# Splitting the rows of maxima with VectorE's tensor_reduce, and sending them in one transfer from ScalarE's queue

## The chip, the cores and the metric

The kernel runs on one core of a Trainium2 chip. A core has five engines with an instruction stream each, in order: TensorE (PE in the profile; its weight loads, PEld, overlap its matmuls), VectorE (DVE), ScalarE (ACT), GpSimd (POOL) and SyncE (SP), which here only issues DMA transfers. ScalarE can issue transfers too; such an issue then stands in ScalarE's stream, between its arithmetic instructions. The metric is the device time of one execution in microseconds; lower is better. Times come from several runs; one execution is also profiled.

## The reference

A transformer block with modulated layer norms: an attention with 16 heads of width 28 over 2048 tokens, and then a gated MLP whose gate is mixed over the tokens by a 2048 x 2048 matrix. Everything is float32.

```python
def _A_ref(x, wqkv, wo):
    B, S, D = x.shape            # 1, 2048, 448
    H = 16
    Dh = D // H                  # 28
    qkv = (x @ wqkv).reshape(B, S, 3, H, Dh).transpose(2, 0, 3, 1, 4)
    q, k, v = qkv[0], qkv[1], qkv[2]
    scores = jnp.einsum("bhqd,bhkd->bhqk", q, k) * (Dh ** -0.5)
    p = _softmax(scores, axis=-1)
    o = jnp.einsum("bhqk,bhkd->bhqd", p, v)
    return o.transpose(0, 2, 1, 3).reshape(B, S, D) @ wo

mod = (_silu(c) @ w_mod).reshape(c.shape[0], 6, 1, -1)
sa, ca, ga, sb, cb, gb = (mod[:, i] for i in range(6))
h = _layernorm(x, axis=-1) * (1 + ca) + sa
x = x + ga * _A_ref(h, A_wqkv, A_wo)
h = _layernorm(x, axis=-1) * (1 + cb) + sb
x = x + gb * _B_ref(h, B_w_in, B_w_sp, B_b_sp, B_w_out)
```

The change concerns the softmax alone: the maximum of each query's scores, which is subtracted before the exponential.

## The kernel before, in words

**Precision.** Operands of the big products are split into a high part in fp32r (a rounded float32 that TensorE multiplies in one pass) and a low part that holds the rest. For q and k of a head the parts are stacked over the partitions, so that one matmul of 128 rows gives the sum of the products.

**The attention.** The stack of a head h lies in `qst[h % 3]` and `kst[h % 3]`, 2048 columns each. Rows 0 to 83 hold the parts of q and k. Rows 84 and 85 of `qst` hold the negated maximum of each query, as a high and a low part, and the matching rows of `kst` hold ones: a score matmul that reads these rows has the maximum already subtracted, and ScalarE only applies exp. `load_head` (L669) loads a head's stack and first writes zeros to rows 84 and 85, because the maxima themselves are taken from the same stack without them.

The steps per head, by their names:

- `m_mm` (L747) computes 128 queries x 512 keys into PSUM (tile mt), and VectorE reduces this to one maximum per query (tile pm, L756). There are 64 of these for a head, or 48 where 4 of 16 blocks are covered by the next step.
- For the heads in `RAW`, 1 to 13, queries 0 to 511 are handled otherwise: `r_mm` (L789) computes their scores (tile rt) with keys on the partitions, ScalarE copies them to SBUF (rawA, rawB, rawC), VectorE keeps a running maximum (rmax, L802), and `r_turn` (L804) transposes rmax on TensorE and reduces it to columns 0 to 3 of tile mxv (L810).
- `m_max` (L760) reduces pm to the rest of mxv, negated, copies it to the high part of tile mxp (rounded to fp32r, L769) and subtracts that for the low part (L770, by the helper `sub` at L143). All three are VectorE instructions on 16 columns.
- `m_fin` (L772) transposes mxp on TensorE (tile mtp, L775), copies the result to SBUF (tile nt, 32 x 128, VectorE, L778) and issues two transfers on the sync queue, of 16 rows of 128 each, into rows 84 and 85 of the head's stack (L780).
- For the heads in `RAW`, `r_neg` (L812) reads those rows: a matmul spreads the negated maxima over all partitions (L814), ScalarE copies this to tile rneg (L818), and GpSimd adds it to each raw tile (`r_sub`, L821), after which ScalarE applies exp (`x_exp`).
- `s_mm` (L833) computes the other scores (st_ps, L786) and their exp (tile P, L831). `pv_mm` (L845) multiplies P with V (o_ps, L850).

**The order.** It is written out by hand. `pair(u)` (L1118) issues two key blocks at a time by a string such as `rrpm|smsmssmsmsm`: r is an `r_mm`, p is `pv_mm` of the pair before and then the steps listed as `late`, | runs the second block's events, s is an `s_mm` and m an `m_mm`. Eight such pairs make a head. `n_o` counts the r and s issued so far in the pair. `m_max` of head h stands among the events at the start of pair 16h - 4, `m_fin` among the late steps in that pair's p, and `r_neg` at the | of the next pair. TensorE, in order, reaches `m_fin`'s transposition right behind the `pv_mm`s of that p.

GpSimd adds, beside the attention, sums of blocks of the mixing matrix (`ws_op`, L946 to L960), whose loads and stores share the sync queue with everything else.

A planner, `Clock` (L1020), chooses which of seven PSUM banks each tile takes: it adds up estimated times of TensorE, ScalarE and VectorE (`clock.read`, `clock.spend`) and picks the bank that comes free first. It changes no order.

Of the kernel before, what the change touches and what calls it, by code (L numbers as in the profile page):

```python
# [8 lines left out]
F32 = mybir.dt.float32  # L9
F32R = mybir.dt.float32r  # L10
AF = mybir.ActivationFunctionType
ALU = mybir.AluOpType
AX = mybir.AxisListType
# [6 lines left out]
NT = S // 128  # L20
# [69 lines left out]
def tile_adaln_mha_gmlp(ctx, tc, x, wqkv, wo, w_in, w_spT, b_sp, w_out, cT, w_mod, out):  # L90
    nc = tc.nc
    ctx.enter_context(tc.manual_schedule())
    pe, dve, act, pool, sp = nc.tensor, nc.vector, nc.scalar, nc.gpsimd, nc.sync
# [48 lines left out]
    def sub(eng, dst, a, hi):  # L142
        eng.tensor_tensor(out=dst, in0=a, in1=hi.bitcast(F32), op=ALU.subtract)  # L143
# [101 lines left out]
    def bank(name):  # L245
        k = mode[0](name) if mode[0] else banks[0]
        banks.remove(k)
        banks.append(k)
        return ring.tile([128, 512], F32, name=name, tag=f"b{k}")
# [6 lines left out]
    def load_mod(pair, eng):  # L256
        for k in range(4):
            n = 2 * D if k < 3 else 512
            wms[pair, k] = wm = e1.tile([128, 2 * D], F32, name="wm", tag=("wm", "wm", "raw")[pair], bufs=4)[:, :n]
            eng.dma_start(wm, w_mod[:, pair, 2 * D * k : 2 * D * k + n])  # L260
            if k < 3:
                wms[pair, k] = wm.rearrange("p (a b) -> p a b", b=D)
# [43 lines left out]
    for r0, r1, a, o in ((0, 128, 0, 3), (0, 64, 3, 1), (64, 128, 3, 1)):  # L306
        b = a + r0 // 64
# [343 lines left out]
    for g in range(1, NG):  # L651
        if g == 3:
# [3 lines left out]
            kst, qst = [a[0] for a in kq], [a[1] for a in kq]  # L656
            npool = att.enter_context(tc.tile_pool(name="npool", bufs=2))
# [73 lines left out]
    RAW = range(1, 14)  # L731
# [13 lines left out]
    pms = {}  # L745

    def m_mm(j, kb):  # L747
        h, t = divmod(j, NT)
        mt = bank("mt")
        pe.matmul(  # L750
            mt, qst[h % 3][:, t * 128 : (t + 1) * 128], kst[h % 3][:, kb * 512 : (kb + 1) * 512], start=True, stop=True
        )
        if h not in pms:
            pms[h] = npool.tile([128, NT, 4], F32, name="pm")
        clock.read("dve", 0.598)
        dve.tensor_reduce(out=pms[h][:, t, kb : kb + 1], in_=mt, axis=AX.X, op=ALU.max)  # L756

    mxs = {}

    def m_max(h):  # L760

        r = 4 if h in RAW else 0
        if h not in mxv:
            mxv[h] = npool.tile([128, NT], F32, name="mxv")
        mx = mxv.pop(h)
        clock.spend("dve", 0.4)
        dve.tensor_reduce(out=mx[:, r:], in_=pms.pop(h)[:, r:, :], axis=AX.X, op=ALU.max, negate=True)
        mxs[h] = npool.tile([128, 2, NT], F32R, name="mxp")
        dve.tensor_copy(mxs[h][:, 0, :], mx)  # L769
        sub(dve, mxs[h][:, 1, :], mx, mxs[h][:, 0, :])  # L770

    def m_fin(h):  # L772
        mx = mxs.pop(h)
        tp = bank("mtp")
        pe.transpose(tp[0 : 2 * NT, 0:128], mx.bitcast(F32).rearrange("p a b -> p (a b)"), ident)  # L775
        nt = npool.tile([2 * NT, 128], F32, name="nt", bufs=1)
        clock.read("dve", 0.3)
        dve.tensor_copy(nt, tp[0 : 2 * NT, 0:128])  # L778
        for i in range(2):
            sp.dma_start(qst[h % 3][84 + i : 85 + i, :].bitcast(F32), nt[NT * i : NT * (i + 1)])  # L780

    mxv, seen, rmax, rneg = {}, [], [], []

# [5 lines left out]
    def r_mm(u):  # L789
        st = score("rt", *divmod(u, NT), 0)  # L790
        b = clock.read("act", 0.477, hold=u % NT > 0)
        act.activation(raw_tile(u), st, AF.Copy)  # L792
        if u % NT:
            seen.append((u, st, b))

    def r_max():
        while seen:
            u, st, b = seen.pop(0)
            if not rmax:
                rmax.append(stage2.tile([128, 512], F32, name="rmax", tag="ql"))  # L800
            clock.read("dve", 0.6, *b)
            dve.tensor_tensor(out=rmax[0], in0=st, in1=raw_tile(u - 1) if u % NT == 1 else rmax[0], op=ALU.max)  # L802

    def r_turn(h):  # L804
        tp = bank("rtp")
        for t in range(4):
            pe.transpose(tp[:, t * 128 : (t + 1) * 128], rmax[0][:, t * 128 : (t + 1) * 128], ident)
        mxv[h] = npool.tile([128, NT], F32, name="mxv")
        clock.read("dve", 0.62)
        dve.tensor_reduce(out=mxv[h][:, 0:4], in_=tp.rearrange("p (a b) -> p a b", b=128), axis=AX.X, op=ALU.max, negate=True)  # L810

    def r_neg(h):  # L812
        st = bank("st_ps")
# [19 lines left out]
    def s_mm(u, qb):  # L833
        st = score("st_ps", *divmod(u, NT), qb)
        clock.ready[u] = clock.read("act", 0.477)[1]
        s_exp(u, qb, st)

    def x_exp(u):
        clock.ready[u] = clock.spend("act", 0.477)
        s_exp(u, 0, raw_tile(u))  # L840
# [4 lines left out]
    def pv_mm(u):  # L845
        h, kt = divmod(u, NT)
        if kt == 0:
            otile[h] = ps_o.tile([128, 512], F32, name="o_ps", tag="o")
        for qb in range(4):
            pe.matmul(  # L850
                otile[h][32 * qb : 32 * qb + 32, :], V[:, kt, h, :], ptiles.pop((u, qb)), start=kt == 0, stop=kt == NT - 1
            )
# [128 lines left out]
    for h in range(H):  # L981
        if h >= 2:
            at(h * NT - LEAD - 10, load_head, h)
        e0 = (h + 1) * NT
        at(e0 + 1, n_copy, h)
        at(e0 + 2, n_sum, h)
        at(e0 + 4, n_recip, h)
        at(e0 + 6, n_bcast, h)
        at(e0 + 8, n_mul, h)
        at(e0 + 9, n_scatter, h)  # L990
        at(h * NT + NT - LEAD, m_max, h)
        at(max(h * NT + NT - LEAD, -2), m_fin, h, when=late)
    for h in RAW:
        at(h * NT - 6, r_turn, h, when=late)
        at(h * NT - 1, r_neg, h)
        for k in range(NT):
            at(h * NT + (k // 2 - 1 if k < 4 else k - 3), r_sub, h * NT + k)
# [114 lines left out]
    def run(when, u):  # L1112
        for fn, a in when.pop(u, []):
            fn(*a)
# [3 lines left out]
    def pair(u):  # L1118
        ss = [[(v, qb) for qb in range(1 if v // NT in RAW else 0, 4)] if v < NU else [] for v in (u, u + 1)]
        S_, M_, R_ = ss[0] + ss[1], m_work[u] + m_work[u + 1], r_work[u] + r_work[u + 1]  # L1120
        X_ = [v for v in (u, u + 1) if v < NU and v // NT in RAW]
        xat = [len(R_) + 4, len(R_) + 6] if u % NT == 0 else [len(R_)] * 2
        if X_:
            order = ORDERS[8 if len(M_) > 6 else 6]
        else:
            lead = 1 if M_ else 4
            order = "r" * len(R_) + "s" * lead + "p" + "ms" * (4 - lead) + "|" + "ms" * 4 + "m" * len(M_)
        n_o = 0

        def exps():  # L1130
            while X_ and n_o >= xat[-len(X_)]:
                x_exp(X_.pop(0))

        run(events, u)
        exps()
        for c in order + "s" * len(S_) + "r" * len(R_) + "m" * len(M_):
            if c == "p":
                if u > 0:
                    pv_mm(u - 2)
                    pv_mm(u - 1)  # L1140
                    clock.pause((u - 2, u - 1))
                run(late, u)
            elif c == "|":
                run(events, u + 1)
            elif c == "s" and S_:
                s_mm(*S_.pop(0))
                n_o += 1
                exps()
            elif c == "r" and R_:
                r_mm(R_.pop(0))  # L1150
                n_o += 1
                exps()
                if not R_:
                    r_max()
            elif c == "m" and M_:
                m_mm(*M_.pop(0))
        assert not X_ and not seen
        run(late, u + 1)
# [102 lines left out]
    h = H - 1  # L1261
# [568 lines left out]
```

## Time and profile before

| What | Value |
|---|---|
| Median of 3 runs | 1381.62 us (1377.2 to 1386.27) |
| Profiled execution, device time | 1383.93 us |
| Its span | 1382.1 us |
| Granted TensorE clock, mean | 0.996 of full |
| TensorE busy | 1353.5 us, 98% |
| VectorE busy | 1099.5 us, 80% |
| ScalarE busy | 907.8 us, 66% |
| GpSimd busy | 603.8 us, 44% |
| 16 instances of the copy at L769 | 0.174 us least, 5.910 us most |
| TensorE's wait at `m_fin`'s transposition (L775) | 15.1 us in 9 heads |
| TensorE's wait for the rows at `r_neg` (L814) | 2.77 us in 1 head |

The shares are of the whole span; the stretch of the change is the attention, from about 130 to 870 us. A row of a timeline gives start, duration, engine, line, operation, output <- input, and in brackets the idle time of the engine just before it with what ended that. Merged rows ("x6") give the time from the first start to the last end. SPq and ACTq are the queues' issues of transfers. The device time of the profiled execution is 1.8 us above its span.

### The profile page before, as it was taken

How to read it: one execution, taken by the hardware profiler on the slowest of the kernel's cores; microseconds unless marked ns; L12 is line 12 of the kernel's file. 1: busy time of each engine (PE TensorE's matmuls, PEld its weight loads, DVE VectorE, ACT ScalarE, POOL GpSimd, SP SyncE). 2: the span in 40 equal slices, each digit the busy share in tenths (PEclk: the TensorE clock that was granted, in tenths of full speed). 3: DMA queues.
4: the chain of work that ended last, by engine and by line, in shares of the span. 5: the costliest groups of instructions: out<-in, count | busy, mean ns of one | idle time of the engine just before them, and what ended most of it. 6: DMA issues, size and time to landing. Idle time of an engine off the chain costs nothing.

```text
span 1382.1 us, 20683 instructions
## 1 busy us (share of the span) xinstructions
PE 1353.5 (98%) x6945; PEld 941.0 (68%) x6945; DVE 1099.5 (80%) x1761; ACT 907.8 (66%) x1687; POOL 603.8 (44%) x521
## 2 busy tenths in 40 slices
PE   9999999999999899989999999999999999999998
PEld 8888555554554455545555554888898888888898
DVE  8898889998998899989998981572168798889682
ACT  6633888998998789879998769464224754444221
POOL 2144447978787778876987772210042000000000
PEclk9999999999999999999999999999999999999999
DMA  8464632455244444434433421533202433325842
GB/s 298 139 176 173 183 91 95 125 149 148 83 120 138 129 118 125 125 101 131 121 111 87 121 77 50 173 134 126 91 1 73 134 99 110 120 92 176 270 162 80
DMA packets 93350, 174.69 MB, mean 126 GB/s; under 512 B 17016, under 2 KB 32250, under 8 KB 90698
## 3 DMA queue, kind: packets, MB, share of 16 engines
q1 hardware_dynamic: 90526, 169.07, 40.5%
q10 hardware_dynamic: 2718, 4.30, 0.9%
q8 instruction: 55, 0.90, 0.3%
q14 instruction: 51, 0.42, 0.1%
HBM read 111.71 MB, written 56.82 MB: 122 GB/s over the span
## 4 chain that ended last, share of the span: by engine, by line
PE 71%; DVE 5%; DMA 1%; ACT 1%; issue 1%; POOL 0%; SPq 0%; ACTq 0%; DVEq 0%; POOLq 0%
PE acc L1606 18%; PE o_ps L850 12%; PE st_ps L786 10%; PE mt L750 10%; PE z_ps L1498 5%; PE z_ps L1330 5%; DVE pm L756 3%; PE wo_ps L1195 3%; PE rt L786 2%; PE y_ps L1684 2%; PE y_ps L1686 2%; PE y_ps L1685 2%; DVE mxp L769 1%; ACT P L831 1%; DMA ws_scr<-ws_raw 1%
## 5 line engine op out<-in xcount | busy, mean ns | idle before, releaser
L756 DVE TENSOR_REDUCE pm<-mt 128x1 f32<-128x512 f32 x816 | 507.2, 680 | 24.2 <-PE mt L750 23.9
L831 ACT ACTIVATE P<-st_ps 128x512 f32<-128x512 f32 x816 | 422.4, 625 | 75.4 <-PE st_ps L786 72.8
L750 PE MATMUL mt<-kst,qst 128*128 128x512 f32 x816 | 333.9, 413 | 0.9 <-DVE rmax L802 0.7
L786 PE MATMUL st_ps<-qst,kst 128*128 128x512 f32 x816 | 300.6, 404 | 2.9 <-ACT P L831 2.9
L850 PE MATMUL o_ps<-P,V 128*32 128x512 f32 x2048 | 249.9, 599 | 1.8 <-ACT P L831 0.4
L1606 PE MATMUL acc<-wsp_h,heapA 128*128 128x512 f32 x752 | 231.7, 389 | 0.0
L750 PEld LDWEIGHTS mt<-kst,qst 128*128 128x128 f32 x816 | 154.5, 189 | 113.2 <-DVE rmax L802 42.2
L958 POOL TENSOR_TENSOR ws_raw<-ws_raw 128x512 f32<-128x512 f32 x124 | 160.0, 1292 | 85.0 <-DMA ws_scr<-ws_raw 66.1
L786 PEld LDWEIGHTS st_ps<-qst,kst 128*128 128x128 f32 x816 | 153.7, 190 | 55.8 <-ACT P L831 8.4
L821 POOL TENSOR_TENSOR rawA<-rawA,rneg 128x512 f32<-128x512 f32 x126 | 160.4, 1293 | 28.7 <-ACT rneg L818 28.7
L1606 PEld LDWEIGHTS acc<-wsp_h,heapA 128*128 128x128 f32 x752 | 141.1, 188 | 29.2
L802 DVE TENSOR_TENSOR rmax<-rt,rmax 128x512 f32<-128x512 f32 x182 | 124.9, 686 | 30.9 <-ACT rawA L792 11.5
L1386 ACT ACTIVATE wsp_h<-raw_sp 128x512 fp32r<-128x512 f32 x104 | 65.6, 632 | 125.7 <-PE acc L1606 110.0
L1606 PE MATMUL acc<-wsp_l,heapA 128*128 128x512 f32 x376 | 146.3, 389 | 0.0
L850 PEld LDWEIGHTS o_ps<-P,V 128*32 128x32 f32 x2048 | 55.8, 109 | 119.7 <-issue 98.0
L821 POOL TENSOR_TENSOR rawB<-rawB,rneg 128x512 f32<-128x512 f32 x64 | 81.8, 1294 | 6.2 <-ACT rneg L818 6.1
L143 DVE TENSOR_TENSOR wsp_l<-raw_sp,wsp_h 128x512 fp32r<-128x512 f32 x104 | 70.2, 684 | 16.7 <-ACT wsp_h L1386 16.4
L1606 PEld LDWEIGHTS acc<-wsp_l,heapA 128*128 128x128 f32 x376 | 70.6, 188 | 14.8
L831 ACT ACTIVATE P<-rawA 128x512 f32<-128x512 f32 x126 | 77.4, 677 | 4.0 <-POOL rawA L821 4.0
L792 ACT ACTIVATE rawA<-rt 128x512 f32<-128x512 f32 x126 | 72.4, 656 | 0.0
L786 PE MATMUL rt<-qst,kst 128*128 128x512 f32 x208 | 69.8, 414 | 0.0
L415 PE MATMUL pq<-heapD,heapD 128*128 128x512 f32 x196 | 61.8, 390 | 0.0
(258 smaller groups left out, 1833.4 us busy)
## 6 DMA issues: line engine op xcount, KB each, us to landing
ws_scr<-ws_raw SPq DMA_DIRECT2D x92, 256.0 KB
raw_sp<-ws_scr SPq DMA_DIRECT2D x92, 256.0 KB
ws_raw<-in_w_spT_dram SPq DMA_DIRECT2D x72, 256.0 KB
kst<-qk_scr SPq DMA_DIRECT2D x45, 224.0 KB
qst<-qk_scr SPq DMA_DIRECT2D x45, 224.0 KB
qk_scr<-qh SPq DMA_DIRECT2D x28, 256.0 KB
qk_scr<-ql SPq DMA_DIRECT2D x28, 256.0 KB
z_scr<-z1t SPq DMA_DIRECT2D x28, 256.0 KB
```

Source lines behind the costliest of these rows:

```text
L143: eng.tensor_tensor(out=dst, in0=a, in1=hi.bitcast(F32), op=ALU.subtract)
L750: pe.matmul(mt, qst[h % 3][:, t * 128 : (t + 1) * 128], kst[h % 3][:, kb * 512 : (kb + 1) * 512], start=True, stop=True)
L756: dve.tensor_reduce(out=pms[h][:, t, kb : kb + 1], in_=mt, axis=AX.X, op=ALU.max)
L786: pe.matmul(st, kst[h % 3][:, kt * 128 : (kt + 1) * 128], qst[h % 3][:, qb * 512 : (qb + 1) * 512], start=True, stop=True)
L792: act.activation(raw_tile(u), st, AF.Copy)
L802: dve.tensor_tensor(out=rmax[0], in0=st, in1=raw_tile(u - 1) if u % NT == 1 else rmax[0], op=ALU.max)
L821: pool.tensor_tensor(out=raw_tile(u), in0=raw_tile(u), in1=rneg[0], op=ALU.add)
L831: act.activation(p, src, AF.Exp, scale=SCALE)
L850: pe.matmul(otile[h][32 * qb : 32 * qb + 32, :], V[:, kt, h, :], ptiles.pop((u, qb)), start=kt == 0, stop=kt == NT - 1)
L958: pool.tensor_tensor(out=ws_tile(op[0]), in0=ws_tile(op[2]), in1=ws_tile(op[4]), op=ALU.add if op[3] == "+" else ALU.subtract)
L1330: pe.matmul(ps_t, w1[:, b, f * 128 : (f + 1) * 128], h2T[g][:, a, :], start=j == 0, stop=j == NST - 1)
L1606: pe.matmul(a[j], z[:, c], w, start=start and k == 0, stop=st == 3 and k == 2, skip_group_check=not new or j == 3)
```

## The change

In `m_max` the tile mxv gets a second column per query block. The copy and the subtraction are replaced by tensor_reduce instructions: one over a single element with `negate` into an fp32r view of the second column, which gives the negated rounded value; one over a single element into the high part, which rounds; and one that adds the two columns, value and negated rounded value, which gives the low part. `r_turn` writes to the first column.

In `m_fin` one transfer of 32 rows of 128 into rows 84 and 85 takes the place of two. For heads 1 to 13 it isn't issued in `m_fin` but kept in a list and issued on ScalarE's queue in `pair`, after an `s_mm` from which on `n_o` is 5 or more. For heads 0, 14 and 15 it is issued in `m_fin` on the sync queue. The planner's entry for `m_max` goes from 0.4 to 0.5.

```diff
         r = 4 if h in RAW else 0
         if h not in mxv:
-            mxv[h] = npool.tile([128, NT], F32, name="mxv")
+            mxv[h] = npool.tile([128, NT, 2], F32, name="mxv")
         mx = mxv.pop(h)
-        clock.spend("dve", 0.4)
-        dve.tensor_reduce(out=mx[:, r:], in_=pms.pop(h)[:, r:, :], axis=AX.X, op=ALU.max, negate=True)
+        clock.spend("dve", 0.5)
+        dve.tensor_reduce(out=mx[:, r:, 0], in_=pms.pop(h)[:, r:, :], axis=AX.X, op=ALU.max, negate=True)
         mxs[h] = npool.tile([128, 2, NT], F32R, name="mxp")
-        dve.tensor_copy(mxs[h][:, 0, :], mx)
-        sub(dve, mxs[h][:, 1, :], mx, mxs[h][:, 0, :])
+        dve.tensor_reduce(out=mx[:, :, 1].bitcast(F32R), in_=mx[:, :, 0:1], axis=AX.X, op=ALU.max, negate=True)
+        dve.tensor_reduce(out=mxs[h][:, 0, :], in_=mx[:, :, 0:1], axis=AX.X, op=ALU.max)
+        with nc.allow_low_precision(reason="the low part of a split, as the other splits write it"):
+            dve.tensor_reduce(out=mxs[h][:, 1, :], in_=mx, axis=AX.X, op=ALU.add)
...
         dve.tensor_copy(nt, tp[0 : 2 * NT, 0:128])
-        for i in range(2):
-            sp.dma_start(qst[h % 3][84 + i : 85 + i, :].bitcast(F32), nt[NT * i : NT * (i + 1)])
+        if h in RAW:
+            turned.append((h, nt))
+        else:
+            m_rows(sp, h, nt)
+
+    turned = []
+
+    def m_rows(eng, h, nt):
+        eng.dma_start(qst[h % 3][84:86, :].bitcast(F32), nt[:, :])
...
-        mxv[h] = npool.tile([128, NT], F32, name="mxv")
+        mxv[h] = npool.tile([128, NT, 2], F32, name="mxv")
...
-        dve.tensor_reduce(out=mxv[h][:, 0:4], in_=tp.rearrange("p (a b) -> p a b", b=128), axis=AX.X, op=ALU.max, negate=True)
+        dve.tensor_reduce(out=mxv[h][:, 0:4, 0], in_=tp.rearrange("p (a b) -> p a b", b=128), axis=AX.X, op=ALU.max, negate=True)
...
             elif c == "s" and S_:
                 s_mm(*S_.pop(0))
                 n_o += 1
+                if n_o >= 5 and turned:
+                    m_rows(act, *turned.pop())
                 exps()
```

## The prediction, made before any run of the change

> **What bounds the kernel now.** I read the page's table of busy time and its chain first, then cut the span into attention heads, then went to the waits of the stretch that the change touches.
>
> ```profile
> PE 1353.5 (98%) x6945; PEld 941.0 (68%) x6945; DVE 1099.5 (80%) x1761; ACT 907.8 (66%) x1687; POOL 603.8 (44%) x521
> ...
> PE 71%; DVE 5%; DMA 1%; ACT 1%; issue 1%; POOL 0%; SPq 0%; ACTq 0%; DVEq 0%; POOLq 0%
> ```
>
> TensorE sets the end: it is busy in 98% of the span and has 71% of the chain. So this change can gain only where TensorE stands still for the rows of maxima. The next view gives the busy time between consecutive starts of m_max's first reduction, that is, one head per row (stretch; length; PE, PEld, DVE, ACT, POOL busy; granted clock; DMA).
>
> ```profile
> 227.77:273.34 45.57, 44.19 (x250) 23.86 (x246) 42.54 (x70) 41.07 (x82) 37.85 (x31) 1.00 0.37 106
> 273.34:317.81 44.47, 44.20 (x250) 23.85 (x246) 41.42 (x71) 41.22 (x82) 33.80 (x27) 1.00 0.49 135
> 317.81:365.00 47.19, 44.29 (x250) 23.84 (x246) 41.14 (x70) 41.18 (x82) 38.81 (x31) 1.00 0.45 134
> 365.00:409.22 44.22, 44.10 (x250) 23.80 (x246) 41.23 (x71) 41.07 (x82) 33.94 (x28) 1.00 0.37 102
> 409.22:456.70 47.48, 45.22 (x250) 23.69 (x246) 41.34 (x70) 41.03 (x82) 37.48 (x31) 1.00 0.48 136
> 456.70:506.39 49.69, 45.18 (x250) 25.22 (x246) 46.00 (x71) 41.34 (x82) 35.88 (x30) 0.97 0.46 126
> 506.39:552.07 45.68, 44.13 (x250) 23.84 (x246) 42.66 (x70) 41.05 (x82) 35.71 (x29) 1.00 0.39 113
> ...
> 597.57:649.30 51.73, 46.00 (x250) 25.92 (x246) 47.32 (x70) 41.43 (x82) 37.05 (x31) 0.93 0.41 119
> 649.30:693.98 44.68, 44.18 (x250) 23.82 (x246) 41.67 (x71) 41.07 (x82) 35.10 (x29) 1.00 0.37 104
> 693.98:738.58 44.60, 44.01 (x251) 23.50 (x243) 41.76 (x70) 40.59 (x81) 36.96 (x30) 1.00 0.37 102
> ```
>
> All these heads hold the same work, but a head takes between 44.22 and 51.73 us. I take 44.5 (the row of 273.34) as a head in which nothing goes wrong. ScalarE and VectorE are busy for 41 us of it, so they have some 3 us of room per head, and TensorE has almost none. What the long heads lost stands in the view of waits and in the view of m_max's instructions (min/median/max in ns).
>
> ```profile
> PE mtp L775 <- DVE mxp L143: 15.1, 9, 5.6
> ```
>
> ```profile
> L767 DVE TENSOR_REDUCE mxv<-pm x16: 202/203/220, 134.8 to 830.1; 128x12 f32<-128x48 f32 x13, 128x16 f32<-128x64 f32 x3
> L769 DVE CAST mxp<-mxv x16: 174/250/5910, 135.0 to 830.3; 128x16 fp32r<-128x16 f32 x16
> L143 DVE TENSOR_TENSOR mxp<-mxv,mxp x16: 174/176/1207, 135.2 to 830.6; 128x16 fp32r<-128x16 f32 x16
> ```
>
> The 16-element CAST takes 174 ns at best and 5,910 at worst, and the subtraction up to 1,207. The reduction ahead of them on the same tile never takes more than 220 ns. The timeline of the two worst heads shows what the CAST waits for.
>
> ```profile
> 456.94 4.71 DVE L769 CAST mxp<-mxv 128x16 fp32r<-128x16 f32 x1
> ...
> 461.92 0.28 PE L775 MATMUL mtp<-ident,mxp 128*32 128x128 f32 x1 [4.40 <-DVE mxp L143]
> ...
> 597.57 0.20 DVE L767 TENSOR_REDUCE mxv<-pm 128x12 f32<-128x48 f32 x1
> 597.81 5.91 DVE L769 CAST mxp<-mxv 128x16 fp32r<-128x16 f32 x1
> ...
> 597.54 1.28 POOL L958 TENSOR_TENSOR ws_raw<-ws_raw 128x512 f32<-128x512 f32 x1
> ...
> 601.20 2.49 POOL L958 TENSOR_TENSOR ws_raw<-ws_raw 128x512 f32<-128x512 f32 x2
> ...
> 603.99 0.39 PE L775 MATMUL mtp<-ident,mxp 128*32 128x128 f32 x1 [5.61 <-DVE mxp L143]
> ...
> 650.50 0.28 PE L775 MATMUL mtp<-ident,mxp 128*32 128x128 f32 x1 [0.39 <-DVE mxp L143]
> ```
>
> The CAST that starts at 597.81 ends at 603.72. GpSimd, which works without a pause from before 597.5, runs out of work at 601.20 + 2.49 = 603.69. So the copy stands until GpSimd is idle. The reduction at 597.57 took its usual 0.20 us while GpSimd worked. TensorE, in order, stands at the transposition behind it.
>
> **The change part by part.**
>
> *Copy and subtraction become tensor_reduce.* What goes is the excess of the long heads over 44.5: 45.57 gives 1.07, 49.69 gives 5.19, 45.68 gives 1.18, 51.73 gives 7.23, 44.68 gives 0.18, 44.60 gives 0.10; together 14.95 us. The two large ones are larger than their waits (4.40 and 5.61) because TensorE comes back slow:
>
> ```profile
> 604.00:610.00 6.00, 6.00 (x19) 4.49 (x23) 5.04 (x9) 3.63 (x7) 0.00 (x0) 0.55 0.30 97
> ...
> 462.00:468.00 6.00, 6.00 (x27) 4.03 (x31) 5.55 (x10) 4.46 (x9) 0.00 (x0) 0.72 0.27 84
> ```
>
> The granted clock is 0.55 in the 6 us after the one wait and 0.72 after the other, and this goes with the waits. The small ones are smaller than their waits (0.18 us lost in the head with 0.39 of wait), so a head takes back about half of a short wait.
>
> What comes: four reductions instead of one and two small operations. Between L767's forms, 16 more elements cost 18 ns, so by estimate a reduction over 16 elements takes 0.17 us and one over 32 takes 0.185. The chain up to the transposition grows by one small step with its gap: 0.17 + 0.04 (from 597.57 + 0.20 to 597.81) = 0.21 us. That can't be below nothing, as an instruction is added, and the most is four times L767's 0.22 in place of three small operations of 0.17 to 0.20, 0.34 more with its gaps. It lies on TensorE's path, since TensorE meets the end of this chain in every head. With half of it taken back: 13 x 0.105 = 1.4 us (ends 0 and 4.4).
>
> That tensor_reduce is free of GpSimd rests on L767's 16 samples, two of them inside the long waits' stretches. What is late next: the maximum over rt and the copy nt, which read PSUM and are behind m_max on VectorE.
>
> *The rows go in one transfer by ScalarE for heads 1 to 13.* One wait goes:
>
> ```profile
> 319.74 0.27 DVE L778 COPY nt<-mtp 32x128 f32<-32x128 f32 x1
> ...
> 324.11 1.21 SPq L780 DMA_DIRECT2D qst<-nt  x2
> ...
> 327.64 0.47 PE L814 MATMUL st_ps<-qst,ones 128*128 128x512 f32 x1 [2.77 <-DMA qst<-nt]
> ```
>
> nt was ready at 320.01, but the sync queue, in order behind the stores of the weight sums, issued at 324.11, and r_neg's matmul waited 2.77 us. That head took 47.19, so 2.69 goes. Of thirteen heads it is the only one with such a wait.
>
> On ScalarE the transfer is issued after the fifth score of the pair, counting the two "r" ahead of the "p": that is the third score behind m_fin. Its cost is bounded by other issues in the trace:
>
> ```profile
> L672 SPq DMA_DIRECT2D qst<-qst x13: 650/662/672, 198.6 to 753.0; - x13
> ```
>
> ```profile
> L891 ACTq DMA_DIRECT2D heapD<-osb x2: 767/1206/1646, 878.0 to 879.7; - x2
> ```
>
> The one issue to the same two rows takes 0.66 us, ScalarE's own from 32 partitions 0.77 at least; I take 0.7. Whether it holds up ScalarE's arithmetic isn't shown; the ends are 0 and 13 x 0.77 = 10 us, and none below nothing, as ScalarE issues nothing there today. The room it has, in an undisturbed head:
>
> ```profile
> 553.59 3.22 ACT L831 ACTIVATE P<-st_ps 128x512 f32<-128x512 f32 x6 [0.29 <-PE st_ps L786]
> ...
> 559.42 0.60 ACT L818 ACTIVATE rneg<-st_ps 128x512 f32<-128x512 f32 x1 [0.58 <-PE st_ps L814]
> ```
>
> ```profile
> 552.81 0.28 PE L775 MATMUL mtp<-ident,mxp 128*32 128x128 f32 x1
> ...
> 558.98 0.40 PE L814 MATMUL st_ps<-qst,ones 128*128 128x512 f32 x1
> ```
>
> ```profile
> PEld st_ps L786 <- DVE pm L756: 0.6, 2, 0.3
> ```
>
> Queued behind the issue stand three exponentials, two copies of r, two exponentials and rneg. rneg has 0.58 us of idle time before it, so 0.12 of the 0.7 is left. TensorE's scores in that stretch wait for banks that VectorE frees (last row), not ScalarE. I take 0.12 x 13 = 1.5 us, nearer to nothing than to 10 because of the 0.58.
>
> Does it land in time? Third exponential done at 553.59 + 1.6 = 555.2. From the two issues at 324.11, the second one began at about 324.7, and r_neg went on at 327.64, so 2.9 us from issue to use: 558.1, and r_neg is due at 558.98. That leaves 0.9 us. Head 13 differs: head 14 isn't in RAW, no "r" is counted, and the issue comes after the fifth score behind m_fin:
>
> ```profile
> 740.37 3.45 ACT L831 ACTIVATE P<-st_ps 128x512 f32<-128x512 f32 x6 [1.53 <-PE st_ps L786]
> ...
> 745.25 0.39 PE L814 MATMUL st_ps<-qst,ones 128*128 128x512 f32 x1
> ```
>
> That is 740.37 + 2.9 + 2.9 = 746.1 against 745.25: a wait of 0.9 us, once. ScalarE won't stand for nt itself: nt is ready at 554.01 + 0.27, before the third exponential ends:
>
> ```profile
> 554.01 0.27 DVE L778 COPY nt<-mtp 32x128 f32<-32x128 f32 x1
> ```
>
> The sync queue is rid of 1.2 us per head and of a stand until nt. No wait of TensorE but the one above is seen to hang on it, so nothing is entered. For heads 0, 14 and 15 one issue on the sync queue replaces two; their rows are not read by an r_neg, so nothing. The planner's 0.5 in place of 0.4 may choose other PSUM banks later on; the trace can't price that, and I put ±1.5 us on it from the half microsecond waits that neighbouring heads differ by.
>
> *Sum.* 14.95 + 2.69 - 1.4 - 1.5 - 0.9 = 13.8 us. The profiled execution took 1383.93 us (its span 1382.1), so 1370.1; that is 11.5 us or 0.8% under the median of the runs, 1381.62. The profiled execution lies 2.3 us above that median; since the waits on GpSimd depend on its phase and are removed, I subtract from the execution in which I counted them.
>
> *A rule against the trace.* The Trainium skill, SBUF — State Buffer, section "Who interferes with whom", says that tensor_reduce on trn2 never contends with GpSimd for the port pair; L767's rows agree. It also says that whoever starts first holds the pair for one whole instruction. The 5.91 us are five instructions of GpSimd, so the trace goes further than that sentence.
>
> **The rivals.**
>
> *The long waits are not all GpSimd's.* If an operation stood for only one GpSimd instruction (1.28 us in the row of 597.54), the rest of the CASTs' 4.71 and 5.91 us would have another cause and stay: 3.4 + 4.6, with the slow clock behind them (51.73 - 44.5 - 5.61 = 1.6 and 0.8) about 10 us, so 1380. Against it: the end at 603.72, 0.03 us behind GpSimd's. The rule above about one whole instruction is what would make it so.
>
> *ScalarE's issue is paid in full.* ScalarE works 41 us of each 44.5, and if all 0.77 us push TensorE each time, 10 instead of 1.5: 1379. For it: six exponentials without a gap. Against: 0.58 idle before rneg.
>
> *Slower: the rows land late.* The transfer waits behind ScalarE's work and lands after r_neg is due, in 13 heads. The slack is 0.9; each microsecond beyond costs 13 us. The gain of 13.8 is used up at 2.0 us after the expected landing (13.8 / 13 + 0.9), and at 3.1 us the kernel is at 1383.9 + 2.2 x 13 - 13.8 = 1399. For it: the fixed place after a score, where the sync queue went as soon as nt was there. Against: even the delayed head's transfer took only 2.9 us.
>
> *GpSimd or the weight sums become the pace.* The long stalls let GpSimd catch up:
>
> ```profile
> 613.21 1.29 POOL L821 TENSOR_TENSOR rawC<-rawC,rneg 128x512 f32<-128x512 f32 x1 [9.52 <-ACT rneg L818]
> ```
>
> Of its 9.52 us idle, the 7.23 us of that head's excess go. The head of 409.22 lost 3.0 us with no wait at m_max; if three more heads do so, 9 us return: 1379.
>
> *More comes.* Added reductions and issues hidden, and the freed sync queue also spares the 3.0 us of the head of 409.22: 1383.9 - 17.6 - 3.0 = 1363.
>
> **How the numbers follow.** Forecast 0.50 (its own range 1366 to 1374), more 0.16, issue paid in full 0.14, GpSimd's pace 0.10, long waits not GpSimd's 0.04, slower 0.06. The predicted time is the forecast's 1370.1. The range reaches from the better case to the issue paid in full, 1362 to 1379, leaving out the last two, part of GpSimd's pace and what lies below. About 1% is what a measurement of this kernel can tell from no change; 1% under the median is 1367.8. The better case and half of the forecast lie below: 0.41. Within 1%: the other half, issue, pace and port: 0.54. Slower: 0.05.
>
> **What would show it.** Right: no DVE operation of m_max above 0.25 us, no wait of TensorE at mtp above 0.5, no granted clock below 1.00 in the heads, all heads near 44.5 to 45. r_neg waiting for qst in head 13 alone shows the landing right. Wrong would be: reductions as long as the CAST was; a wait at r_neg in most heads; exponentials behind the issue late, and TensorE's scores waiting for ScalarE; or new waits of exponentials on GpSimd.

## The result, and the profile after

| Kernel | Median, us | Range, us | Ratio to before, 95% interval |
|---|---|---|---|
| Before, runs beside the changed kernel | 1380.39 | 1377.2 to 1386.27 | 1 |
| Changed | 1364.74 | 1363.54 to 1367.31 | 0.9884, 0.9847 to 0.9922 |

The changed kernel is faster: the ratio in the table stands for 1.16%, and the medians lie 15.6 us apart. Its profiled execution took 1367.31 us, the slowest of its four; beside the profiled execution of before, 1383.93, it is 16.6 us shorter. The runs of the changed kernel lie within 3.8 us of each other, those of before within 9.1.

The page of the changed kernel, busy time and chain by engine:

```profile
PE 1351.7 (99%) x6945; PEld 938.8 (69%) x6945; DVE 1084.3 (79%) x1777; ACT 907.9 (66%) x1687; POOL 604.0 (44%) x521
...
PE 89%; POOL 3%; DMA 2%; DVE 2%; ACT 2%; issue 1%; SPq 0%; ACTq 0%; DVEq 0%; POOLq 0%
```

VectorE has 16 instructions more and is busy for 15.2 us less. What it was "busy" with before was partly standing still inside an instruction. TensorE's share of the chain went from 71% to 89%.

The view of the instructions on mxv and mxp, changed kernel (min/median/max in ns): the three reductions that took the place of the copy and the subtraction.

```profile
L769 DVE TENSOR_REDUCE mxv<-mxv x16: 170/171/180, 135.5 to 814.3; 128x16 fp32r<-128x16 f32 x16
```

```profile
L770 DVE TENSOR_REDUCE mxp<-mxv x16: 158/160/171, 135.6 to 814.4; 128x16 fp32r<-128x16 f32 x16
L772 DVE TENSOR_REDUCE mxp<-mxv x16: 185/186/188, 135.7 to 814.6; 128x16 fp32r<-128x32 f32 x16
```

No instance is over 0.19 us, against 5.91 and 1.21 before. TensorE's wait for them, in the view of waits of the changed kernel, is 1.1 us where it was 15.1, and the two that remain belong to heads 13 and 14, where it had stood before the change too (0.34 and 0.70 us):

```profile
PE mtp L777 <- DVE mxp L772: 1.1, 2, 0.7
```

The heads of the changed kernel, from one start of m_max to the next (columns as in the prediction):

```profile
183.25:229.07 45.82, 45.11 (x253) 24.28 (x249) 41.31 (x72) 40.24 (x81) 30.90 (x25) 1.00 0.34 94
229.07:273.30 44.23, 44.10 (x250) 23.88 (x246) 41.24 (x72) 41.15 (x82) 37.90 (x31) 1.00 0.39 110
...
317.50:361.69 44.19, 44.07 (x250) 23.85 (x246) 41.20 (x72) 41.16 (x82) 38.81 (x31) 1.00 0.48 141
...
405.85:453.04 47.19, 45.23 (x250) 23.71 (x246) 41.35 (x72) 41.12 (x82) 37.05 (x30) 1.00 0.46 134
453.04:497.26 44.22, 44.08 (x250) 23.93 (x246) 41.23 (x71) 41.11 (x82) 36.07 (x29) 1.00 0.49 141
...
541.45:589.95 48.50, 45.94 (x250) 24.10 (x246) 41.43 (x72) 41.20 (x82) 40.24 (x33) 0.96 0.46 132
589.95:634.14 44.19, 44.05 (x250) 23.84 (x246) 41.22 (x71) 41.15 (x82) 34.62 (x28) 1.00 0.48 128
```

The heads that took 49.69 and 51.73 us now take 44.22 and 44.19, and the one whose rows had waited in the sync queue went from 47.19 to 44.19. Nearly all heads are now alike at 44.2. Two are long: that of 405.85, as long as before (47.48), and that of 541.45, which was 45.50 before. Head 1 (183.25) went from 44.99 to 45.82. In sum the twelve heads from 183.25 to 722.32 take 539.07 us, where they took 555.80 from 182.78 to 738.58: 16.7 us, all of the difference.

### The profile page after: what moved, and what is told of

Read it like the earlier page. It is cut to its first block, busy times and chain, and to the rows that moved or that the text cites. A ratio compares the mean times of both kernels' runs of the same rounds, so it can differ in the third digit from the quotient of the medians.

```text
span 1365.5 us, 20681 instructions
## 1 busy us (share of the span) xinstructions
PE 1351.7 (99%) x6945; PEld 938.8 (69%) x6945; DVE 1084.3 (79%) x1777; ACT 907.9 (66%) x1687; POOL 604.0 (44%) x521
## 4 chain that ended last, share of the span: by engine, by line
PE 89%; POOL 3%; DMA 2%; DVE 2%; ACT 2%; issue 1%; SPq 0%; ACTq 0%; DVEq 0%; POOLq 0%
PE acc L1617 19%; PE o_ps L859 15%; PE mt L750 13%; PE st_ps L795 12%; PE z_ps L1509 5%; PE z_ps L1341 5%; PE pq L415 4%; PE rt L795 3%; PE wo_ps L1206 3%; DMA ws_scr<-ws_raw 2%; PE y_ps L1696 2%; PE y_ps L1697 2%; PE pv L397 2%; PE y_ps L1695 2%; ACT P L840 1%
## 5 line engine op out<-in xcount | busy, mean ns | idle before, releaser
L143 DVE TENSOR_TENSOR wsp_l<-raw_sp,wsp_h 128x512 fp32r<-128x512 f32 x104 | 70.4, 686 | 16.6 <-ACT wsp_h L1397 16.4
```

## The experiments

The theory (A): the copy and the subtraction of m_max stood for GpSimd, and that was nearly all of the gain. The rival (B): the place of the rows' transfer in the queues carries it. Further: what a transfer's issue costs ScalarE, and what the two long heads wait for.

| Kernel | Median, us | Range, us | Ratio to before, 95% interval |
|---|---|---|---|
| Reductions only (rows as before) | 1366.44 | 1363.95 to 1368.31 | 0.9913, 0.9893 to 0.9933 |
| ScalarE's transfer only | 1375.60 | 1371.67 to 1382.32 | 0.9990, 0.9972 to 1.0008 |
| Reductions, one transfer on the sync queue | 1363.79 | 1363.10 to 1364.63 | 0.9893, 0.9873 to 0.9914 |
| Copy as a reduction, subtraction kept | 1372.70 | 1366.50 to 1376.40 | 0.9948, 0.9928 to 0.9967 |
| Before, with short sums on GpSimd | 1360.03 | 1359.39 to 1360.56 | 0.9864, 0.9844 to 0.9885 |
| Changed, rows sent twice | 1408.15 | 1405.99 to 1412.16 | 1.0219, 1.0197 to 1.0241 |
| Changed, rows in two issues on ScalarE | 1369.45 | 1368.37 to 1372.61 | 0.9936, 0.9917 to 0.9954 |
| Changed, later loads of heads 8 and 11 | 1376.05 | 1374.81 to 1377.53 | 0.9975, 0.9960 to 0.9989 |
| The same with the rows on the sync queue | 1375.86 | 1372.71 to 1377.88 | 0.9975, 0.9960 to 0.9990 |
| Changed, a spare tile for two sums | 1359.48 | 1359.17 to 1360.47 | 0.9866, 0.9840 to 0.9892 |
| The same with the rows on the sync queue | 1360.23 | 1358.77 to 1360.55 | 0.9868, 0.9842 to 0.9894 |
| Changed, 128 copies added | 1391.98 | one run | none |

The runs of before beside these experiments have medians of 1378.1 to 1379.5 us and lie between 1372.3 and 1386.4.

### The two halves alone

Reductions only:

```diff
-        if h in RAW:
-            turned.append((h, nt))
-        else:
-            m_rows(sp, h, nt)
+        for i in range(2):
+            sp.dma_start(qst[h % 3][84 + i : 85 + i, :].bitcast(F32), nt[NT * i : NT * (i + 1)])
```

> The changed kernel with the rows issued as before: two transfers on the sync queue. Theory A (the copy and the subtraction waited for GpSimd, and that was nearly all of the gain): no operation of m_max over 0.25 us, no wait of TensorE at mtp over 0.5, 13 to 15 us under before, about 1366 to 1368; a wait of 2 to 3 us for the rows may stand at r_neg in one head. Theory B (the move to ScalarE's queue carries the gain): at most 5 us under before, about 1375 to 1380.

ScalarE's transfer only is the kernel before with the other half of the diff: copy and subtraction as they were, one transfer in the list `turned`.

> The kernel before with the one transfer on ScalarE's queue alone; copy and subtraction stay. Theory A: the CASTs still take up to 4 to 6 us in some heads, and the time is 0 to 3 us under before, 1377 to 1380. Theory B: 10 us or more under before, about 1368. A cost of ScalarE's issues paid in full (13 x 0.65) would show as 5 us above before.

By their ratios the reductions alone gave 0.87%, where the whole change gave 1.16%, and the runs of these two kernels overlap; the transfer alone has a ratio whose interval holds 1. The reductions alone lie 11.7 us under before by the medians, a little less than the 13 to 15 that were expected. In their profile one wait for the rows was left, 1.50 us in the head of 316.18. So theory A holds and B falls. In the profile of the second, the instructions on mxp read:

```profile
L769 DVE CAST mxp<-mxv x16: 174/540/1198, 134.9 to 820.3; 128x16 fp32r<-128x16 f32 x16
L143 DVE TENSOR_TENSOR mxp<-mxv,mxp x16: 174/176/1274, 135.1 to 820.8; 128x16 fp32r<-128x16 f32 x16
```

One thing was expected otherwise: this execution has no CAST of 4 to 6 us. The median CAST is longer than in the profile of before (540 against 250 ns), the longest far shorter (1.2 against 5.9). The runs of this kernel spread over 10.7 us. Its timeline shows what each instruction stands for:

```profile
318.96 1.28 POOL L965 TENSOR_TENSOR ws_raw<-ws_raw 128x512 f32<-128x512 f32 x1 [2.53 <-issue]
319.07 1.20 DVE L769 CAST mxp<-mxv 128x16 fp32r<-128x16 f32 x1
320.19 1.26 POOL L828 TENSOR_TENSOR rawB<-rawB,rneg 128x512 f32<-128x512 f32 x1
320.30 1.19 DVE L143 TENSOR_TENSOR mxp<-mxv,mxp 128x16 fp32r<-128x16 f32 x1
```

The copy ends at 320.27, 0.03 us behind the end of one GpSimd instruction (320.24), and the subtraction at 321.49, as far behind the end of the next (321.45). In this profile and that of before, every copy and subtraction over 0.2 us ends 0.02 to 0.04 us behind the end of a GpSimd instruction, wherever the rows show that end by itself.

One transfer on the sync queue for every head:

```diff
-        if h in RAW:
-            turned.append((h, nt))
-        else:
-            m_rows(sp, h, nt)
+        m_rows(sp, h, nt)
```

> The changed kernel with the one transfer of a head on the sync queue instead of ScalarE's. If only the number of issues mattered: as the changed kernel, 1364 to 1366. If the place in the sync queue matters: a wait of 2 to 3 us at r_neg in one or two heads, 1366 to 1368.

At 1363.79 us it equals the changed kernel. In its profile the one wait for the rows is 0.98 us (head 4), which ScalarE's queue avoids; head 1 in turn takes 44.98 where the changed kernel takes 45.82, since there ScalarE's issue, 1.27 us long, held up its exponentials. The queue is therefore worth nothing that can be seen here. Against two transfers on the sync queue, one gave 2.7 us by the medians, but the runs of the two kernels overlap and their profiled executions differ by 1.05 us; the wait for the rows went from 1.50 to 0.98.

### Is it GpSimd, and for how long does an instruction stand?

Only the copy becomes a reduction; the subtraction stays on two SBUF tiles:

```diff
-        dve.tensor_copy(mxs[h][:, 0, :], mx)
+        dve.tensor_reduce(out=mxs[h][:, 0, :], in_=mx.rearrange("p (a o) -> p a o", o=1), axis=AX.X, op=ALU.max)
```

> The kernel before with only the copy written as a tensor_reduce; the subtraction stays a tensor_tensor on two SBUF tiles. If such a subtraction stands for one GpSimd instruction at most: none over 1.3 us, half of the gain or more, 1367 to 1373. If it stands until GpSimd is idle, as the copy did: subtractions of 4 to 6 us in the heads where the copy took that long, 1377 to 1381.

```profile
L769 DVE TENSOR_REDUCE mxp<-mxv x16: 170/170/171, 135.2 to 816.5; 128x16 fp32r<-128x16 f32 x16
L143 DVE TENSOR_TENSOR mxp<-mxv,mxp x16: 174/260/1290, 135.4 to 816.7; 128x16 fp32r<-128x16 f32 x16
```

About half of the gain: the reduction is free, and the subtraction stands for one GpSimd instruction at most (1.29 us) in this execution. Both replaced instructions had stood.

Now GpSimd's load is taken away from the kernel before, which keeps its copy and its subtraction. Its sums of weight blocks run over 8 columns instead of 512, so most of the mixing matrix is left out, and their tile is filled with zeros once:

```diff
             ws_raw.append(dpool.tile([128, 7, 512], F32, name="ws_raw", tag="heapF"))
+            pool.memset(ws_raw[0], 0.0)
...
-                out=ws_tile(op[0]), in0=ws_tile(op[2]), in1=ws_tile(op[4]), op=ALU.add if op[3] == "+" else ALU.subtract
+                out=ws_tile(op[0])[:, 0:8],
+                in0=ws_tile(op[2])[:, 0:8],
+                in1=ws_tile(op[4])[:, 0:8],
+                op=ALU.add if op[3] == "+" else ALU.subtract,
```

> The kernel before, with its copy and subtraction and its two transfers, but GpSimd's sums of weight blocks run over 8 columns instead of 512, so most of the mixing matrix is left out and GpSimd has 124 x 1.2 us less to do. If GpSimd's work is what the copy waits for: no CAST over 1.3 us, few over 0.25, heads of 44.2 to 44.6, and 1355 to 1366. If the copy waits for something else: CASTs of 4 to 6 us stay and the heads keep their lengths, 1375 or more.

```profile
L769 DVE CAST mxp<-mxv x16: 174/175/943, 134.8 to 807.2; 128x16 fp32r<-128x16 f32 x16
L143 DVE TENSOR_TENSOR mxp<-mxv,mxp x16: 174/175/177, 135.0 to 807.5; 128x16 fp32r<-128x16 f32 x16
```

With GpSimd mostly free, the same two instructions take 175 ns in the median and 0.94 us at most, heads 1 to 12 take 44.0 to 45.0 us, and the kernel 1360.0. The runs lie within 1.2 us of each other. So GpSimd's work is what they stood for, and with it went the spread of the runs. For the two copies of 4.71 and 5.91 us this profile alone would not do, as the profile of ScalarE's transfer alone had none either; what ties those two to GpSimd is their ends, 461.65 and 603.72, 0.03 us behind the last of a row of GpSimd instructions (461.62 and 603.69). The run also gives a mark for a kernel that GpSimd hardly holds up: about 1360 us.

For the length of one wait, the changed kernel got a copy of 16 columns between two SBUF tiles at the start of each pair, used by nothing:

```diff
-    dpool.tile([128, 104], F32, name="padD")
+    padD = dpool.tile([128, 104], F32, name="padD")
...
+        dve.tensor_copy(padD[:, 0:16].bitcast(F32R), ident[:, 0:16])
         run(events, u)
         exps()
```

> The changed kernel with one more VectorE copy of 16 columns between two SBUF tiles, used by nothing, at the start of each of the 128 pairs. If a copy waits for the GpSimd instruction in flight and no more: all 128 between 0.17 and 1.3 us. If it waits until GpSimd is idle whenever GpSimd works on: many of 2 to 6 us. If both happen: a few long ones among many short ones, and the place in GpSimd's instruction at which the long ones start tells whether that decides.

```profile
L1143 DVE CAST padD<-ident x128: 109/426/1359, 145.3 to 851.5; 128x16 fp32r<-128x16 f32 x128
```

None of 128 is longer than about one GpSimd instruction, so a copy normally stands for the one in flight. The 4.71 and 5.91 us of the profile before, over four and five GpSimd instructions, are real but rare: 2 of its 16, none of 16 in the profile of ScalarE's transfer alone, none of these 128. The place in GpSimd's instruction alone doesn't decide it. The CAST of 5.91 us began 0.27 us after a start of GpSimd's; in the profile of ScalarE's transfer alone one began 0.28 us after a start (593.56 against 593.28) and took 1.05. What makes a copy miss four or five gaps in a row stays open.

### What an issue costs ScalarE

```diff
-                    m_rows(act, *turned.pop())
+                    for _ in range(2):
+                        m_rows(act, *turned[-1])
+                    turned.pop()
```

> The changed kernel with each of the 13 transfers on ScalarE's queue issued twice. If an issue costs ScalarE's 0.65 us on TensorE's path: 8 us more than the changed kernel, 1372 to 1374. If it is taken up by ScalarE's idle time before rneg, which is 0.25 us in the changed kernel: 13 x 0.4 at most, 1364 to 1370. If the issue runs beside ScalarE's arithmetic: no change, 1363 to 1366.

This run doesn't measure what it was meant to. Both transfers write the same rows, and two issues took 2.90 us here where two to different rows take 1.17 (below): the second waits, I take it, for the first to land. Timeline of ScalarE in one head:

```profile
281.24 2.90 ACTq L789 DMA_DIRECT2D qst<-nt  x2
284.23 1.58 ACT L840 ACTIVATE P<-st_ps 128x512 f32<-128x512 f32 x3 [2.50 <-DVE pm L756]
```

It is a measurement of another thing: ScalarE stood for 2.50 us per head, a head took 48 instead of 44.2 us, and in most heads the granted clock fell to 0.96. That is where the 43 us over the changed kernel come from. An issue on ScalarE behind a wait of 2.5 us would thus have cost nearly three times what the change gains.

The clean form sends each row by its own transfer, so that none waits:

```diff
-                    m_rows(act, *turned.pop())
+                    h, nt = turned.pop()
+                    for i in range(2):
+                        act.dma_start(qst[h % 3][84 + i : 85 + i, :].bitcast(F32), nt[NT * i : NT * (i + 1)])
```

> The changed kernel with two transfers per head on ScalarE's queue, one for each row, so that none waits for the other: 13 issues more of about 0.6 us. If an issue is on TensorE's path: 5 to 8 us above the changed kernel, 1370 to 1373. If ScalarE's idle time takes it up only in part: 1366 to 1369. If it runs beside ScalarE's arithmetic: 1363 to 1367.

ScalarE's timeline around the issue, first in the changed kernel, then with two issues:

```profile
542.99 1.74 ACT L840 ACTIVATE P<-st_ps 128x512 f32<-128x512 f32 x3 [0.31 <-PE st_ps L795]
544.21 0.65 ACTq L789 DMA_DIRECT2D qst<-nt  x1
544.97 1.58 ACT L840 ACTIVATE P<-st_ps 128x512 f32<-128x512 f32 x3 [0.24 <-DVE pm L756]
...
548.80 0.60 ACT L827 ACTIVATE rneg<-st_ps 128x512 f32<-128x512 f32 x1 [0.25 <-PE st_ps L823]
```

```profile
544.76 1.76 ACT L840 ACTIVATE P<-st_ps 128x512 f32<-128x512 f32 x3 [0.29 <-PE st_ps L795]
546.03 1.17 ACTq L1160 DMA_DIRECT2D qst<-nt  x2
547.30 1.58 ACT L840 ACTIVATE P<-st_ps 128x512 f32<-128x512 f32 x3 [0.78 <-DVE pm L756]
```

With one issue, it starts at 544.21, while the third exponential still runs to 544.73, and the next begins 0.24 us later than it could (the bracket names VectorE, but the issue is what ends just before). ScalarE has 0.25 us left before rneg, where it had 0.58 before the change, and TensorE loses nothing: 6.17 us lie between mtp and r_neg's matmul (542.20 to 548.37), as before the change (552.81 to 558.98). With two issues the gap is 0.78, the reserve is gone, and a head takes 44.6 instead of 44.2 us. So the first issue is free in this head, and in heads 2 to 12 alike (6.15 to 6.17 us from mtp to r_neg). In head 1 it is not: there the issue takes 1.27 us, and mtp to r_neg takes 8.59 us, where it took 7.75 before; in head 13 it is 6.16 and was 5.99. The second issue costs 0.4 us per head, 4.7 us in all.

### The two long heads that are left

In the head of 405.85, the chain of the changed kernel reads:

```profile
421.35 3.55 DMA kst<-qk_scr
424.91 8.95 DMA ws_scr<-ws_raw
...
435.25 1.30 POOL rawA L830
...
437.11 0.59 ACT P L840
```

GpSimd's timeline has the wait:

```profile
434.00 1.29 POOL L967 TENSOR_TENSOR ws_raw<-ws_raw 128x512 f32<-128x512 f32 x1 [7.59 <-DMA ws_scr<-ws_raw]
```

GpSimd waits for the store of a sum to land, because the next sum goes into the same tile; the raw tiles for the exponentials are behind it in GpSimd's stream. The store was issued behind the loads of head 8. In the head of 541.45 GpSimd waits for such a store in the same way, 6.02 us until 574.61. My first guess was to move those loads:

```diff
-            at(h * NT - LEAD - 10, load_head, h)
+            at(h * NT - LEAD - (6 if h in (8, 11) else 10), load_head, h)
```

> The changed kernel with the load of heads 8 and 11 moved four blocks later, off the slots 98 and 146 where loads and stores of the weight sums stand in the sync queue. If those sums, late behind the head's load, make the two long heads that are left (47.2 and 48.5 us): heads 6 and 9 fall to about 44.2 to 45 and the time to 1357 to 1361. If not: the two heads stay, 1363 to 1367; if the later load is itself awaited, a new wait of TensorE on qst or kst and more than 1367.

> The one transfer of a head on the sync queue, and the load of heads 8 and 11 four blocks later. If both hold: 1356 to 1360. If the rows wait behind the moved loads in the sync queue: a wait at r_neg of 1 us or more in one or two heads, 1360 to 1364.

Both miss. The two heads became longer (52.82 and 50.77 in the first), since the next head's first rt matmul, which reads the stack whose load had been moved, now waited. The profile names a transfer of the sync queue as what ended each wait, which is inferred; that it was the moved load isn't shown:

```profile
PE rt L795 <- DMA heapD<-osb: 7.0, 1, 7.0
PE rt L795 <- DMA ws_scr<-ws_raw: 4.1, 1, 4.1
```

So these loads can't stand four blocks later. The other way is not to wait for the store's landing. The sums of slots 99 to 101 and 149 to 150 were built in tile 6, free at that time, instead of tile 0 (only these parts of the string W_SUMS are shown):

```diff
-99:0=1-3 100:3=w2.2,0=0-2 101:1=4+5,-1,p24.1=0
+99:6=1-3 100:3=w2.2,6=6-2 101:1=4+5,-1,p24.1=6
...
-149:0=2+4,-0 150:3=w15.3,2=1-2,p15.3=0
+149:6=2+4,-6 150:3=w15.3,2=1-2,p15.3=6
```

> The changed kernel with the same sums of weight blocks, but at slots 99 to 101 and 149 to 150 they are built in a tile that is free then, instead of in the one whose store was issued a slot before. If GpSimd's wait for that store's landing (up to 9 us, behind the loads of head 8 or 11) makes the two long heads that are left: heads 6 and 9 fall from 47.2 and 48.5 to 44.2 to 45.5, and the time to 1358 to 1361. If the wait is for something else in the sync queue: no change, 1363 to 1367.

> The same, with each head's one transfer on the sync queue instead of ScalarE's. As the one before within 1.5 us if the queue doesn't matter; if ScalarE's place does matter, a wait of 1 to 3 us at r_neg in one or two heads and so much more.

```profile
405.23:449.39 44.16, 44.04 (x250) 23.85 (x246) 41.20 (x71) 41.19 (x82) 39.91 (x32) 1.00 0.51 150
...
537.76:582.31 44.55, 44.33 (x246) 23.66 (x242) 41.23 (x72) 40.79 (x82) 38.11 (x31) 1.00 0.46 133
```

Heads 6 and 9 fall to 44.16 and 44.55 us, and the kernel to 1359.48, 5.3 us under the changed kernel and at the mark of the short sums. With the rows on the sync queue it is the same within 0.8 us. This version beats both kernels.

## Why the prediction was right, and where its size was off

The prediction named 1370.1 us with 1362 to 1379. The measured median, 1364.74, lies inside, 5.4 us under 1370.1; the profiled execution, 1367.31, lies 2.8 under. It gave 0.41 to faster by over 1% and 0.54 to within 1%; the measured 1.16% lies just beyond that line, and its interval reaches to both sides of it. (Its chances for within 1% add up to 0.53, not 0.54, and slower has 0.06 in one list and 0.05 in the other.) The mechanism was right; the two gains in its sum were put too small and its three costs too large. That the total came as near as it did is partly luck: the gain that was missing from the sum was in part given back by one head that became longer, below.

- *What goes with the copy and the subtraction* (14.95 us by the excess of six heads over 44.5). The same six heads became shorter by 16.9 us. An undisturbed head was put at 44.5 and is 44.2, as the row of 365.00 (44.22) in the prediction could have told; the head that served as the measure had a copy of 0.44 us in it. From this too low a loss the prediction read that a head takes back about half of a short wait. Against 44.2 it takes back nothing: the head with the wait of 0.39 us (649.30) had lost 0.5.
- *The added reduction* (1.4 us). It costs nothing that can be seen. In the changed kernel m_max starts at 541.45 and TensorE takes up the transposition at 542.20, 0.75 us, as in the undisturbed head before (552.07 to 552.81, 0.74). From the start of m_max to the end of its last instruction it takes 0.64 us, where it took 0.62. The small reductions start 0.09 to 0.12 us apart, not 0.21:

```profile
541.69 0.17 DVE L769 TENSOR_REDUCE mxv<-mxv 128x16 fp32r<-128x16 f32 x1
541.78 0.16 DVE L770 TENSOR_REDUCE mxp<-mxv 128x16 fp32r<-128x16 f32 x1
541.90 0.19 DVE L772 TENSOR_REDUCE mxp<-mxv 128x16 fp32r<-128x32 f32 x1
```

  L772 starts 0.21 us behind L769, whose result it reads, as the subtraction started 0.21 behind the copy whose result it read (552.31 and 552.52). L770 doesn't read L769's result, and L772 doesn't read L770's, so the added instruction fits into that gap.

- *ScalarE's issue* (1.5 us). In heads 2 to 12 the 0.58 us of idle time before rneg did cover it, as was argued, and more fully, since it runs beside the exponential ahead of it. Heads 1 and 13 lost 0.83 and 0.19 us. Two issues showed how near the edge that is.
- *The wait in the sync queue* (2.69 us) went, in the head where it stood: 47.19 to 44.19. What became of the 2.77 us of wait step by step: 1.50 with the reductions and two transfers on the sync queue, 0.98 with one transfer there, none on ScalarE's queue. So one transfer less is worth some 0.5 of it, and the place in the queue the last 1.0; why the wait was already shorter with the reductions alone isn't shown.
- *The wait in head 13* (0.9 us) didn't come. The transfer was issued at 726.45, and r_neg's matmul started at 729.17 without a wait. The step that failed is the place: I let the issue begin when the fifth exponential ends, and it began as that exponential starts (726.48). The landing was a little shorter as well, at most 2.72 us from issue to use where 2.9 were taken.
- *The rivals.* "More comes" came in its first half, the hidden costs; the sync queue's relief did nothing for the head of 405.85 (47.19). "GpSimd's pace" came in one head of the profiled execution, 45.50 to 48.50, with GpSimd waiting for the landing of a store of the weight sums, and gave back 3.0 us; this and the 0.83 of head 1 are why the sum of the gains, 16.9 + 3.0 and 0.6 in the other heads, comes to 16.7. "Slower" and "the issue paid in full" fell by the 6.17 us between mtp and r_neg. "The long waits are not all GpSimd's" fell with the copies: no small instruction of m_max in the changed kernel takes more than 0.22 us.
- *The signs.* The instructions of m_max stayed under 0.25 us, as foretold. Four signs did not hold: head 14 kept a wait of 0.70 us at mtp, head 9 had a granted clock of 0.96, heads 1, 6 and 9 took 45.82, 47.19 and 48.50 us, and head 13 had no wait for its rows.
- *One whole instruction or until idle.* From two waits in one execution I took it that a copy stands until GpSimd is idle. The Trainium skill, SBUF — State Buffer, section "Who interferes with whom", says one whole instruction. The 128 copies of at most 1.36 us agree with it; the 4.71 and 5.91 us don't, and there the measurement decides. The forecast counted its gain in an execution that happened to have the two long ones and subtracted it from that execution; the runs beside the experiments have medians of 1378.1 to 1379.5, some 5 us under it. That the time came out near all the same is luck in part.

## What to carry to other kernels

A tiny VectorE instruction whose longest instance is many times its shortest is probably standing for something: look at what GpSimd does at that moment, and whether the instruction can be written as one that doesn't stand, such as tensor_reduce here. The gain then lies as much in the spread of the times as in their median. Before an instruction is added, see whether it reads what the one ahead of it writes: here one that doesn't fitted into a gap and cost nothing. ScalarE took one transfer's issue nearly for free, with 0.58 us of idle time before its next awaited result; a second issue, or one that waits, was paid by everyone behind it.

## What the runs showed of the hardware that was not expected

- Both a copy and a subtraction on SBUF tiles of 16 columns stand for a GpSimd instruction in flight (up to 1.36 and 1.29 us); tensor_reduce never did in 64 instances of the changed kernel (0.22 us at most), of which 40 lie wholly within a row of GpSimd's work.
- A copy can stand over four or five GpSimd instructions, 4.71 and 5.91 us, though this is rare.
- Of three small reductions on VectorE, the one that needs neither of the others' results starts 0.09 us behind the first; the one that needs the first's result starts 0.21 behind it.
- ScalarE begins to issue a transfer while its preceding exponential runs: the issue at 544.21 began 0.52 us before that exponential's end.
- A store that had been issued needed 8.95 us to land behind another head's loads, and the wait for it, three engines away, was TensorE's.
